# Summing landmark parities on GpSimd from partition-shifted ScalarE copies, in place of two TensorE parity matmuls per batch

## The chip, the cores and the metric

The kernel runs on one core of one Trainium2 chip. The metric is the device time of one execution in microseconds (us). A run counts as slow when it takes over 1.5% longer than the fastest run of the same kernel, and is left out of comparisons. The profile is one execution recorded by the hardware profiler; its span is about 2 us shorter than its quoted time, so I compare spans with spans and times with times.

Engine names as the profile has them: PE is TensorE (matmuls), PEld its weight loads, DVE is VectorE, ACT is ScalarE, POOL is GpSimd, SP is SyncE.

## The reference, cut to what matters

```python
B, H, S, D, m = 8, 8, 576, 64, 32              # batches, heads, rows, head size, landmarks
q_lm = q.reshape(B, H, m, S // m, D).mean(axis=3)      # landmark = mean of 18 consecutive rows
k_lm = k.reshape(B, H, m, S // m, D).mean(axis=3)
A, Bm, C = sm(q, k_lm), sm(q_lm, k_lm), sm(q_lm, k)    # sm: scaled scores, softmax
Z = ...                                        # six iterations towards an inverse of Bm
x = A @ Z @ C @ v                              # as [4608, 512]
out = (((x @ w1) * (x @ w2)) @ w3) @ w_out
```

The inputs are fp32, and so is the output, [4608, 512].

## The kernel before: the parts that the change touches

A tile `qkT` holds q and k with the head dimension and the *parity of the row* along the 128 partitions: partitions 0 to 63 have the even rows and 64 to 127 the odd ones. Each landmark averages even and odd rows, so two steps make it: sums along the free axis (`landmarks`, on GpSimd), and one addition of the two partition halves. The kernel before does this addition on TensorE, at the head of `attention`. It splits the fp32 sums into an fp16 high and low part, multiplies both by a stacked identity `iit`, and ScalarE casts the product to `lm`.

```python
    def landmarks(st, t, eng=nc.gpsimd, pieces=iter(())):
        # ... x = st["qkT"][:, t, hs, :, :]: free-axis sums, six halves and thirds
        eng.tensor_tensor(out=tr, in0=x[:, :, 0, :], in1=x[:, :, 1, :], op=ALU.add)   # L183
        eng.tensor_tensor(out=tr, in0=tr, in1=x[:, :, 2, :], op=ALU.add)              # L184
        eng.tensor_tensor(out=o, in0=t3[:, :, :, 0], in1=t3[:, :, :, 1], op=ALU.add)  # L189
        eng.tensor_tensor(out=o, in0=o, in1=t3[:, :, :, 2], op=ALU.add)               # L190
        eng.tensor_copy(out=hi, in_=o)                                                # L191
        eng.tensor_tensor(out=lo, in0=o, in1=hi, op=ALU.subtract)                     # L192

    def attention(st, bank=None):
        psL = small()
        for i in range(2):
            nc.tensor.matmul(psL[:, :], iit..., parts[:, i]..., ...)                  # L201
        nc.scalar.copy(out=lm, in_=pl)                                                # L206
        nc.gpsimd.tensor_tensor(out=qbd, in0=lm..., in1=par..., op=ALU.mult)          # L208
        yield
        psB = bank()
        # ... first product of two landmark tiles, psB <- lm, lm                      # L217
        # ... (cut: scores, softmaxes, six iterations)
        psZ = small()                                                                 # L404
        # ... psZ <- xd, bmbd
        nc.scalar.activation(out=zt[:, 0], in_=pzv, func=AXF.Copy, scale=-ZS)         # L409
        nc.vector.scalar_tensor_tensor(out=zt[:, 1], in0=pzv, ...)
        normalise(1)                     # VectorE writes the second ahat             # L370
        yield
        # expanded products psG <- zt, wup (L425), evicted to gt by ScalarE (L429) and VectorE
    def up(st, j, w):                    # matmul gt x ahat (L439) into a big() of PSUM (3 buffers)
        # w == 0: ScalarE evicts it to a_sb (L443); w == 1: VectorE multiplies it with a_sb
    def down(ab, b0, t0, half, hold, bank):   # matmuls (L457); ScalarE evicts to o_sb (L466)

    for b in range(B):
        for j in range(8):
            up(st, j, 0); steps(at, (1, 1, 1, 0, 1, 0, 1, 0)[j]); up(st, j, 1)   # cut
        nxt = attention(sts[b + 2], acc)
        for n in range(nd):              # nd = 8 for even b, 10 for odd b
            down(...)
            steps(at)                    # batch b+1's attention proceeds between down products
        steps(at, 30)
        at = nxt
```

At the program's start, PE also multiplies two weights, w3 and w_out: it turns (transposes) blocks of w3 (`w3f`), ScalarE and VectorE evict them as high and low parts (`w3t`, L495 and L496), and PE multiplies these (L503). To *evict* means to copy a product out of PSUM, where PE leaves it.

In these traces each engine takes its instructions in program order, so what stands at the head of an engine's queue delays all that follow on it: the `w3t` eviction that VectorE starts at 26.77 us before the change starts at 30.07 after it, when the sums put in front of it have ended. I call the end of a batch and the beginning of the next the *batch change*. There are six of them in the steady state (those with `b + 2 < B`), three after 8 down steps and three after 10.

The softmax here doesn't subtract the row's maximum and nothing guards it: scores larger than these inputs give would overflow.

## Time and profile before

| before | value | read from |
|---|---|---|
| time, median of 3 | 283.61 us (283.22 to 288.74, the last a slow run) | timed runs |
| span of the profiled run | 281.0 us | profile page |
| PE busy | 269.0 us, 96% | profile page |
| PE on the chain that ended last | 84% | profile page |
| PE's listed waits | 6.5 us, 1.6 of them pauses marked "issue" | list of waits |

The page of the kernel before gives the span, the busy time of each engine (share of the span, number of instructions) and the chain of work that ended last, by engine:

```profile
span 281.0 us, 9504 instructions
...
PE 269.0 (96%) x3996; PEld 152.0 (54%) x3996; DVE 161.8 (58%) x423; ACT 128.9 (46%) x235; POOL 161.7 (58%) x210
...
PE 84%; POOL 4%; ACT 4%; issue 3%; DVE 1%; DMA 1%; ACTq 0%; DVEq 0%; POOLq 0%
```

PE bounds this kernel: it is nearly always busy, and the last work to end hangs on it. The other engines are busy about half the time, but whether they can take more depends on the place. PE's list of waits, before (engine, line, releaser: total us, times, longest us):

```profile
PE big L439 <- ACT a_sb L443: 1.4, 7, 0.2
PE acc L328 <- issue: 1.3, 1, 1.3
...
PE small L201 <- POOL parts L191: 0.8, 1, 0.8
```

In the steady state PE waits only in short stretches of 0.2 us for `a_sb`. The wait for `parts`, and a second of 0.4 us just behind it, are at the start, near 34 us, where the first landmarks come late.

ScalarE's timeline of one batch change, before (start us, duration us, engine, line, operation, out<-in, and in brackets the idle time ahead of it):

```profile
200.89 0.60 ACT L466 ACTIVATE o_sb<-acc 128x512 f32<-128x512 f32 x1 [2.11 <-PE acc L457]
201.38 0.27 ACT L409 ACTIVATE zt<-small 128x128 f16<-128x128 f32 x1
...
205.02 1.02 ACT L429 ACTIVATE gt<-big 128x1024 f16<-128x1024 f32 x1
206.04 0.64 ACT L443 CAST a_sb<-big 128x576 f16<-128x576 f32 x1
```

Although ScalarE is only 46% busy, two short passages have no gap: `zt` starts 0.49 us after an `o_sb` eviction that takes 0.60 us (the two overlap), and the first `a_sb` starts as the last `gt` ends. PE's timeline of the same batch change:

```profile
200.78 0.44 PE L404 MATMUL small<-bmbd,xd 128*64 128x128 f32 x4
...
205.34 0.66 PE L439 MATMUL big<-ahat,gt 128*128 128x288 f16 x4
205.84 0.59 PE L201 MATMUL small<-parts,iit 128*128 128x512 f16 x2
206.27 1.14 PE L439 MATMUL big<-ahat,gt 128*128 128x288 f16 x8
207.34 0.22 PE L217 MATMUL acc<-lm 64*32 64x32 f16 x8
```

The two parity matmuls (L201) occupy PE from 205.84 to 206.27, 0.43 us. This listing also defines the *stage*, from the start of `psZ` (L404, 200.78) to the first landmark product (L217, 207.34). It is 6.56 us here, and has two parts: to the first up product (205.34), 4.56 us, and from there to the landmark product, 2.00 us.

### The profile page before, as it was taken

The numbers are of one execution on the slowest core, as the hardware profiler recorded it, in microseconds if no ns is written. First come the engines' busy times: TensorE is split into PE (matmuls) and PEld (weight loads), VectorE is DVE, ScalarE is ACT, GpSimd is POOL, SyncE is SP. The second block draws the span as 40 slices with busy tenths as digits, with TensorE's granted clock in tenths as the row PEclk, the third lists the DMA queues.
The fourth block names the chain that finished last, engine by engine and source line by source line (L and its number), as shares of the span: only waits on it lengthen the run. The fifth ranks groups of instructions, "written<-read, shape, count | busy, mean of one in ns | idle before, by whom it ended". The sixth has DMA issues, their size and how long they took to land.

```text
span 281.0 us, 9504 instructions
## 1 busy us (share of the span) xinstructions
PE 269.0 (96%) x3996; PEld 152.0 (54%) x3996; DVE 161.8 (58%) x423; ACT 128.9 (46%) x235; POOL 161.7 (58%) x210
## 2 busy tenths in 40 slices
PE   7999899999999998999999999999999999999993
PEld 3456355444673475447645754574468346734741
DVE  7743134644476675656765765576576755766710
ACT  2643245133662574157427732672276246615531
POOL 1717935396279749944897599459947953500000
PEclk9999999999999999999999999999999999999997
DMA  7999999999717996997699969995999452014024
GB/s 220 322 229 252 203 279 161 161 273 160 128 36 158 224 187 103 160 250 160 134 179 228 159 143 213 227 163 112 222 176 160 124 157 77 5 40 109 6 75 112
DMA packets 61979, 45.57 MB, mean 162 GB/s; under 512 B 35569, under 2 KB 54001, under 8 KB 61937
## 3 DMA queue, kind: packets, MB, share of 16 engines
q1 hardware_dynamic: 47280, 31.93, 48.5%
q0 software_dynamic: 13824, 11.54, 29.8%
q10 hardware_dynamic: 832, 1.51, 1.6%
q8 instruction: 31, 0.51, 0.8%
q14 instruction: 12, 0.09, 0.1%
HBM read 38.80 MB, written 9.44 MB: 172 GB/s over the span
## 4 chain that ended last, share of the span: by engine, by line
PE 84%; POOL 4%; ACT 4%; issue 3%; DVE 1%; DMA 1%; ACTq 0%; DVEq 0%; POOLq 0%
PE big L439 23%; PE acc L457 13%; PE big L457 11%; PE acc L503 10%; PE big L382 6%; PE big L425 5%; ACT a_sb L443 2%; PE small L323 2%; PE big L367 2%; PE acc L323 2%; PE big L490 2%; PE big L242 2%; PE small L503 1%; DMA w3f<-in_moe_w_dram 1%; PE big L292 1%
## 5 line engine op out<-in xcount | busy, mean ns | idle before, releaser
L439 PE MATMUL big<-ahat,gt 128*128 128x288 f16 x512 | 72.2, 286 | 2.0 <-ACT a_sb L443 1.4
L445 DVE TENSOR_TENSOR ab<-a_sb,big 128x576 f16<-128x576 f16 x64 | 48.0, 750 | 27.6 <-PE big L439 15.2
L439 PEld LDWEIGHTS <-gt 128*128 128x128 f16 x512 | 48.4, 98 | 20.3 <-issue 5.6
L443 ACT CAST a_sb<-big 128x576 f16<-128x576 f32 x64 | 40.9, 639 | 32.0 <-PE big L439 31.9
L503 PE MATMUL acc<-wsp,w3t 128*128 128x512 f16 x168 | 40.5, 379 | 0.8 <-ACT w L506 0.5
L457 PE MATMUL acc<-w,ab 128*128 128x512 f16 x160 | 40.3, 381 | 0.0
L457 PEld LDWEIGHTS <-ab 128*128 128x128 f16 x288 | 24.0, 98 | 29.0 <-issue 4.2
L457 PE MATMUL big<-w,ab 128*128 128x512 f16 x128 | 32.7, 381 | 0.0
L466 ACT ACTIVATE o_sb<-acc 128x512 f32<-128x512 f32 (+1 forms) x20 | 11.7, 587 | 42.2 <-PE acc L457 40.6
L183 POOL TENSOR_TENSOR tr<-qkT 128x768 f32<-128x768 f16 x16 | 26.3, 1642 | 7.3 <-DMA qkT<-qkn 7.3
L253 POOL TENSOR_TENSOR t<-ect 96x384 f32<-96x384 f32 x16 | 15.9, 995 | 24.3 <-ACT ect L246 16.3
L503 PEld LDWEIGHTS <-w3t 128*128 128x128 f16 x192 | 18.1, 98 | 20.6 <-issue 1.8
L431 DVE TENSOR_SCALAR gt<-big 128x1024 f16<-128x1024 f32 x16 | 19.6, 1225 | 14.8 <-PE big L425 14.8
L184 POOL TENSOR_TENSOR tr<-tr,qkT 128x768 f32<-128x768 f32 x16 | 26.3, 1642 | 1.3
L208 POOL TENSOR_TENSOR qbd<-lm,par 128x512 f16<-128x512 f16 x8 | 8.3, 1042 | 26.3 <-ACT lm L206 26.3
L429 ACT ACTIVATE gt<-big 128x1024 f16<-128x1024 f32 x16 | 16.4, 1025 | 11.9 <-PE big L425 11.9
L496 DVE SCALAR_TENSOR_TENSOR w3t<-big,w3t 128x512 f16<-128x512 f32 x16 | 11.0, 690 | 17.1 <-ACT w3t L495 17.1
L466 ACT ACTIVATE o_sb<-big 128x512 f32<-128x512 f32 x16 | 9.6, 597 | 18.5 <-PE big L457 18.5
L425 PE MATMUL big<-wup,zt 64*32 64x512 f16 x512 | 17.4, 380 | 0.1
L495 ACT ACTIVATE w3t<-big 128x512 f16<-128x512 f32 x16 | 9.5, 594 | 11.8 <-PE big L490 11.8
L246 ACT ACTIVATE ect<-big 96x768 f32<-96x768 f32 x16 | 12.9, 807 | 3.6 <-PE big L242 2.9
L190 POOL TENSOR_TENSOR o<-o,tr 128x256 f32<-128x256 f32 x16 | 12.9, 807 | 1.3
(317 smaller groups left out, 373.0 us busy)
## 6 DMA issues: line engine op xcount, KB each, us to landing
vt<-in_v_dram SPq DMA_DIRECT2D x28, 288.0 KB, 4.3
out_dram<-o_sb SPq DMA_DIRECT2D x23, 192.0 KB, 3.6
qkn<-in_k_dram POOLq DMA_DIRECT2D x12, 288.0 KB, 5.7
qkn<-in_q_dram POOLq DMA_DIRECT2D x12, 288.0 KB, 6.2
w3f<-in_moe_w_dram SPq DMA_DIRECT2D x6, 512.0 KB, 7.8
out_dram<-o_sb SPq DMA_DIRECT2D x24, 128.0 KB, 3.5
wup<-in_moe_w_dram POOLq DMA_DIRECT2D x4, 512.0 KB, 32.9
out_dram<-o_sb SPq DMA_DIRECT2D x24, 64.0 KB, 3.5
```

The costliest lines, as they stand in the source:

```text
L183: eng.tensor_tensor(out=tr, in0=x[:, :, 0, :], in1=x[:, :, 1, :], op=ALU.add)
L184: eng.tensor_tensor(out=tr, in0=tr, in1=x[:, :, 2, :], op=ALU.add)
L382: nc.tensor.matmul(psI[32 * t:32 * t + 32, qd, o:96], tz_[sl, qd, :], sz_[sl, qd, o:96], start=True, stop=True, tile_position=(32 * h, 32 ...
L425: nc.tensor.matmul(psG[32 * h:32 * h + 32, qd, :], zt[rs, i, h, :], wup[rs, h, w, fs], start=(i == 0), stop=(i == 1), tile_position=(64 * ...
L429: nc.scalar.activation(out=g[:, :, w, fs], in_=psG, func=AXF.Copy, scale=1.0 / ZS)
L431: nc.vector.tensor_scalar(out=g[:, :, w, fs], in0=psG, scalar1=1.0 / ZS, scalar2=None, op0=ALU.mult)
L439: nc.tensor.matmul(p[:, c, 0:HS], st["g"][:, qd, w, 128 * j:128 * j + 128], st["ahat"][qd][:, c, :], start=(qd == 0), stop=(qd == 1))
L443: nc.scalar.copy(out=st["a_sb"], in_=p[:, :, 0:HS])
L445: nc.vector.tensor_tensor(out=st["ab"][:, j, st["t0"]:st["t0"] + S].rearrange("p (c s) -> p c s", c=2), in0=st["a_sb"], in1=p[:, :, 0:HS], ...
L457: nc.tensor.matmul(pso[:, :], ab[:, j, t0:t0 + 128], w34[:, j, :], start=(j == 0), stop=(j == 7))
L466: nc.scalar.activation(out=o_sb[:, c], in_=pso[:, c], func=AXF.Copy, scale=1.0 / (X64 * X64))
L503: nc.tensor.matmul(psW[j][:, :], turned[j, c // 4][:, a, c % 4, :], wsp[:, b, c, :], start=(c == 0 and a + b == 0), stop=(c == 7 and a == 1))
```

## The change

The intent is to take the parity matmuls off the busiest engine. Two ScalarE copies swap the partition halves of the fp32 sums into a tile `far`, and one GpSimd addition `o + far` gives `lm` at once, in both halves. The high/low split, the PSUM tile and the cast from PSUM go. The shifts are placed where the sums are ready: k after the sixth `down` of a batch, q at the batch's end. At the start, VectorE takes half of the heads of batch 0's q sums from GpSimd, which was late there.

The core of the diff, with cuts marked:

```diff
-            eng.tensor_copy(out=hi, in_=o)
-            eng.tensor_tensor(out=lo, in0=o, in1=hi, op=ALU.subtract)
+    def sums(st, t, shared=False, pieces=iter(())):
+        # ... o = st["o"][t], the four additions as before
+        work = ((nc.gpsimd, 0, 4), (nc.vector, 4, 4)) if shared else ((nc.gpsimd, 0, H),)
+        # ...
+    def landmarks(st, t):
+        o = st["o"][t]
+        far = pz.tile([128, H, 32], FP32, name="far", bufs=1)
+        nc.scalar.copy(out=far[0:64], in_=o[64:128])
+        nc.scalar.copy(out=far[64:128], in_=o[0:64])
+        # ...
+        nc.gpsimd.tensor_tensor(out=lm[:, t], in0=o, in1=far, op=ALU.add)
+        if t == 0:  # ... qbd as before
@@ attention
-        psL = small()
-        for i in range(2):
-            nc.tensor.matmul(psL[:, :], iit..., parts[:, i]..., ...)
-        nc.scalar.copy(out=lm, in_=pl)
@@ start
-        landmarks(sts[0], 0)
+        sums(sts[0], 0, shared=True)
         load_w3(5)
         steps(fd, 4)
+        landmarks(sts[0], 1)
         # ...
-        steps(fd, 6)
+        steps(fd, 3)
+        landmarks(sts[0], 0)
+        steps(fd, 4)
@@ batch loop
-        nxt = attention(sts[b + 2], acc) if b + 2 < B else iter(())
         for n in range(nd):
             # ... down(...)
+            if b + 2 < B and n == 5:
+                landmarks(sts[b + 2], 1)
             steps(at)
         steps(at, 30)
-        at = nxt
+        if b + 2 < B:
+            landmarks(sts[b + 2], 0)
+            at = attention(sts[b + 2], acc)
```

More of the change, by code (lines that the diff above doesn't have):

```diff
@@ L137, in constants @@
         eye = consts.tile([128, 2, 32], FP32, name="eye")
-        iit = consts.tile([128, 2, 64], FP16, name="iit")
         onesq = consts.tile([128, 2, 4, 2, 4], FP16, name="onesq")
@@ L146, in constants @@
             nc.vector.memset(par[sl, i:i + 1], 1.0)
-            for jj in range(2):
-                nc.vector.tensor_copy(out=iit[sl, jj, :], in_=ident[sl, sl])
         for h in range(4):
@@ L171, in constants @@
         nc.vector.tensor_tensor(out=eye2, in0=eye, in1=eye, op=ALU.add)
-        return mask4, par, ones, eye2, iit, onesq, selc, lomask
-    def landmarks(st, t, eng=nc.gpsimd, pieces=iter(())):
-        if "parts" not in st:
-            st["parts"] = pz.tile([128, 2, 2, H, 32], FP16, name="parts")
-        for h0 in ((0,) if eng is nc.gpsimd else (0, 4)):
-            own, n = ("", H) if eng is nc.gpsimd else ("v", 4)
+        return mask4, par, ones, eye2, onesq, selc, lomask
+    def sums(st, t, shared=False, pieces=iter(())):
+        if "o" not in st:
+            st["o"] = {}
+        o = st["o"][t] = pz.tile([128, H, 32], FP32, name="o%d" % t, bufs=1)
+        work = ((nc.gpsimd, 0, 4), (nc.vector, 4, 4)) if shared else ((nc.gpsimd, 0, H),)
+        for eng, h0, n in work:
+            own = "" if eng is nc.gpsimd else "v"
             hs = slice(h0, h0 + n)
             x = st["qkT"][:, t, hs, :, :]
-            tr = pat.tile([128, n, NP], FP32, name="tr" + own, bufs=1)
+            tr = pat.tile([128, 4 if own else H, NP], FP32, name="tr" + own, bufs=1)[:, 0:n]
             eng.tensor_tensor(out=tr, in0=x[:, :, 0, :], in1=x[:, :, 1, :], op=ALU.add)
@@ L186, in landmarks @@
             t3 = tr.rearrange("p h (l g) -> p h l g", g=3)
-            o = pat.tile([128, n, 32], FP32, name="o3" + own, bufs=1)
-            hi, lo = st["parts"][:, 0, t, hs, :], st["parts"][:, 1, t, hs, :]
-            eng.tensor_tensor(out=o, in0=t3[:, :, :, 0], in1=t3[:, :, :, 1], op=ALU.add)
-            eng.tensor_tensor(out=o, in0=o, in1=t3[:, :, :, 2], op=ALU.add)
-            eng.tensor_copy(out=hi, in_=o)
-            eng.tensor_tensor(out=lo, in0=o, in1=hi, op=ALU.subtract)
-            next(pieces, None)
+            eng.tensor_tensor(out=o[:, hs], in0=t3[:, :, :, 0], in1=t3[:, :, :, 1], op=ALU.add)
@@ new lines, in sums @@
+            eng.tensor_tensor(out=o[:, hs], in0=o[:, hs], in1=t3[:, :, :, 2], op=ALU.add)
+            next(pieces, None)
+    def landmarks(st, t):
[3 more added lines that the diff above has]
+        nc.scalar.copy(out=far[64:128], in_=o[0:64])
+        if "lm" not in st:
+            st["lm"] = pat.tile([128, 2, H, 32], FP16, name="lm")
+        lm = st["lm"]
+        nc.gpsimd.tensor_tensor(out=lm[:, t], in0=o, in1=far, op=ALU.add)
+        if t == 0:
+            qbd = st["qbd"] = pat.tile([128, H, 2, 32], FP16, name="qbd")
+            nc.gpsimd.tensor_tensor(
+                out=qbd,
+                in0=lm[:, 0, :, :].unsqueeze(2).to_broadcast([128, H, 2, 32]),
+                in1=par.unsqueeze(1).unsqueeze(3).to_broadcast([128, H, 2, 32]),
+                op=ALU.mult)
@@ L196, in attention @@
     def attention(st, bank=None):
         bank = bank or small
-        qkT, vt, parts = st["qkT"], st["vt"], st["parts"]
-        psL = small()
-        for i in range(2):
-            nc.tensor.matmul(psL[:, :], iit.rearrange("p a d -> p (a d)"),
-                             parts[:, i].rearrange("p t h l -> p (t h l)"),
-                             start=(i == 0), stop=(i == 1))
-        pl = psL.rearrange("p (t h l) -> p t h l", t=2, l=32)
-        lm = pat.tile([128, 2, H, 32], FP16, name="lm")
@@ L206, in attention @@
-        nc.scalar.copy(out=lm, in_=pl)
-        qbd = pat.tile([128, H, 2, 32], FP16, name="qbd")
-        nc.gpsimd.tensor_tensor(
-            out=qbd,
-            in0=lm[:, 0, :, :].unsqueeze(2).to_broadcast([128, H, 2, 32]),
-            in1=par.unsqueeze(1).unsqueeze(3).to_broadcast([128, H, 2, 32]),
-            op=ALU.mult)
-        yield
+        qkT, vt, lm, qbd = st["qkT"], st["vt"], st["lm"], st["qbd"]
         psB = bank()
@@ L576 @@
         load_weight(1, moe_w2)
-        mask4, par, ones, eye2, iit, onesq, selc, lomask = constants()
+        mask4, par, ones, eye2, onesq, selc, lomask = constants()
         fd = fold(pf, wof, w3f, wsp, warm_up)
@@ L593 @@
         turn_on_pe(sts[0], 1, 4, nc.vector.tensor_copy)
-        landmarks(sts[0], 1)
+        sums(sts[0], 1)
         steps(fd, 5)
@@ L597 @@
         turn_on_pe(sts[0], 0, 4, nc.vector.tensor_copy)
-        landmarks(sts[0], 0)
+        sums(sts[0], 0, shared=True)
         load_w3(5)
         steps(fd, 4)
+        landmarks(sts[0], 1)
         load_w3(6)
         turn_all(1)
-        steps(fd, 6)
+        steps(fd, 3)
+        landmarks(sts[0], 0)
+        steps(fd, 4)
         at = attention(sts[0])
-        for n, m in enumerate((2, 2, 2, 3, 3, 2, 1, 1, 1, 1, 2, 2, 3, 3)):
+        for n, m in enumerate((2, 2, 3, 3, 2, 2, 1, 1, 1, 2, 2, 3, 3)):
             steps(at)
-            if n == 1:
+            if n == 0:
                 load_w3(7)
-            elif n == 4:
+            elif n == 3:
                 pieces = qk_pieces(sts[2], 2)
-                landmarks(sts[1], 1, pieces=pieces)
-                landmarks(sts[1], 0, pieces=pieces)
-            if 3 < n < 8:
-                load_v_piece(sts[1], 1, n - 4, ident[0:NP, 0:1])
+                sums(sts[1], 1, pieces=pieces)
+                sums(sts[1], 0, pieces=pieces)
+            if 2 < n < 7:
+                load_v_piece(sts[1], 1, n - 3, ident[0:NP, 0:1])
             steps(fd, m)
         steps(at, 30)
+        landmarks(sts[1], 1)
+        landmarks(sts[1], 0)
         steps(fd, 64)
@@ L631 @@
             up(st, j, 0)
-            steps(at, (1, 1, 1, 0, 1, 0, 1, 0)[j])
+            steps(at, (0, 1, 1, 0, 1, 0, 1, 0)[j])
             if b + 2 < B and j > 5:
@@ L637 @@
                 pieces = qk_pieces(sts[b + 3], b + 3) if b + 3 < B else iter(())
-                landmarks(sts[b + 2], 1, pieces=pieces)
-                landmarks(sts[b + 2], 0, pieces=pieces)
+                sums(sts[b + 2], 1, pieces=pieces)
+                sums(sts[b + 2], 0, pieces=pieces)
         steps(at, 1)
-        nxt = attention(sts[b + 2], acc) if b + 2 < B else iter(())
         hold = {}
```

## The prediction

> **What bounds it now.** TensorE: busy 269.0 of the 281.0 us span (the page), 84% of the chain that ended last. PE's waits on other engines sum to about 6 us (list of waits). Only PE time, or a new PE wait, counts. ScalarE (46%), VectorE and GpSimd (58%) have slack on average, not at each place.
>
> **What goes, comes, moves.**
> - PE: two 128x512 parity matmuls per batch go. In the timeline they push the next matmul from 205.84 to 206.27: 0.43 us, 3.4 us in eight batches.
> - ScalarE: the 595 ns lm cast goes; four 64x256 shifts per batch come, of which the trace has none. The Trainium skill ("ScalarE: Activation LUTs", What ACT_TABLE_LOAD costs) gives 186 ns + 0.833 ns per element, neighbours overlapping by 93 ns; the trace's 96x1 copy at 183 ns agrees. Estimate: 0.4 us each, 0.7 us a pair.
> - GpSimd: per parity 397 + 672 ns (cast, subtract) go, one add (about 0.67 us) comes.
> - VectorE: half the q sums of batch 0, about 1.5 us once.
>
> **Start.** PE waited 0.77 + 0.37 us for the sums at 34 us. Now they should be ready about 33.4, and PE needs them about 34.4: 1.57 us gained with the two matmuls. But the w3 block that PE turns at 41.75 was issued at 23.5 and took 17.8 us, landing about 41.3; an earlier PE then waits. I count 0.9 (0.5 to 1.5). Batch 1, shifted well ahead, gains its 0.43.
>
> **Steady state: 0.43 gained, more given back, at two places in each of six batch changes.**
> 1. The k shifts stand between an o_sb eviction and zt on ScalarE. zt slips from 201.38 to about 202.0; VectorE takes zt, then ahat, in order, so the second ahat ends about 203.25, not 202.63. The second expanded product (L425) takes its PSUM buffer, at 202.86: a new PE wait near 0.4 us.
> 2. The q shifts stand before the first a_sb of the next batch. Chain: shifts 0.7, GpSimd add 0.67, first landmark product. After an 8-chunk batch a_sb slips about 0.6 us, and the third up product needs its buffer: PE reaches the landmark product about 0.4 us later than before, the removed matmuls counted. After a 10-chunk batch that product waits for the add: about 0.24 us later.
> Sum: 3 x (0.42 + 0.37) + 3 x (0.42 + 0.24) = about 4.3 us lost.
>
> **Net.** -0.9 - 0.4 + 4.3 = +3; shaded, since waits may overlap, to +2.3. Predicted 285.9 us against 283.6; eight times in ten 282.4 to 288.6. Faster by over 2%: 0.01; within 2%: 0.94; slower by over 2%: 0.05.
>
> **What would show each step.**
> - PE busy falls by about 3.4 us or more, yet the span doesn't; the list of waits gains PE waits behind ScalarE's a_sb, VectorE's ahat and GpSimd's lm, 0.2 to 0.9 us each, six times ahat, three each the others.
> - Shifts near 0.4 us, pairs just ahead of zt and of a batch's first a_sb in ScalarE's timeline.
> - The first landmark product 0.2 to 0.4 us later after the last down product.
> - At 34 us no PE wait for GpSimd; perhaps one for w3f near 40 us.
>
> **What would make it wrong.** Shifts much shorter than 0.4 us: both steady waits fade, and the kernel gains about 3 us. Slack at ahat that I don't see would do half of that. Shifts or adds slowed by shared SBUF traffic (VectorE and GpSimd summing together at the start) would make it worse; the landing of w3f decides the start.

## More of the kernel before

The line numbers shift: L404, L409, L425, L439, L443, L457, L466, L217 and L496 of before are L401, L406, L422, L436, L440, L454, L463, L214 and L493 after. The shifts are L193 and L194, the addition L198, and the sums L182 to L187.

## The result, and the profile after

The changed kernel took 291.01, 290.81 and 291.43 us in three fast runs and 302.56 us in a slow one (clock 0.975), median of all four 291.22 us. The kernel before took a median of 283.71 us in the same rounds. Ratios here and below are the mean time of one kernel's fast runs over that of the other's of the same rounds, so not quite the ratio of the medians that I quote. The ratio is 1.0266, 95% interval 1.0241 to 1.029: slower by over 2%, and outside the predicted range.

The page after:

```profile
span 289.2 us, 9473 instructions
...
PE 268.8 (93%) x3980; PEld 150.1 (52%) x3980; DVE 164.6 (57%) x423; ACT 138.4 (48%) x259; POOL 155.1 (54%) x194
...
PE 72%; ACT 10%; DVE 5%; POOL 5%; issue 4%; DMA 1%; ACTq 0%; POOLq 0%; DVEq 0%
```

PE has fallen from 84% of the chain to 72%, and ScalarE, VectorE and GpSimd have taken its place. ScalarE's busy share rose by only two points. PE's list of waits, after:

```profile
PE big L436 <- ACT a_sb L440: 4.0, 10, 0.9
PE acc L214 <- POOL lm L198: 2.9, 3, 1.0
PE acc L500 <- DVE w3t L493: 2.0, 2, 1.7
PE big L422 <- DVE ahat L367: 1.5, 6, 0.3
PE big L422 <- ACT zt L406: 1.5, 6, 0.2
```

What is new comes in threes and sixes, at the six batch changes: of the ten waits for `a_sb`, seven are the short ones of before, and three, of 0.86 us each, are new. The `w3t` wait is at the start. ScalarE's timeline of the same batch change, after:

```profile
204.87 0.60 ACT L463 ACTIVATE o_sb<-acc 128x512 f32<-128x512 f32 x1 [2.11 <-PE acc L454]
205.49 0.40 ACT L193 COPY far<-o 64x256 f32<-64x256 f32 x1
205.90 0.41 ACT L194 COPY far<-o 64x256 f32<-64x256 f32 x1
206.33 0.28 ACT L406 ACTIVATE zt<-small 128x128 f16<-128x128 f32 x1
...
209.87 1.02 ACT L426 ACTIVATE gt<-big 128x1024 f16<-128x1024 f32 x1
210.92 0.40 ACT L193 COPY far<-o 64x256 f32<-64x256 f32 x1
211.34 0.40 ACT L194 COPY far<-o 64x256 f32<-64x256 f32 x1
211.76 0.64 ACT L440 CAST a_sb<-big 128x576 f16<-128x576 f32 x1
```

Both passages without a gap have been cut open. `zt` now starts 1.46 us after `o_sb`, where it was 0.49: the pair of copies inserts 0.97 us. The first `a_sb` starts 0.87 us after `gt` ends, where it was 0. Look at the starts: each copy begins only when what stands before it has ended (204.87 + 0.60 = 205.47, and the copy starts at 205.49), and `zt` after it likewise. PE's timeline, after:

```profile
204.76 0.44 PE L401 MATMUL small<-bmbd,xd 128*64 128x128 f32 x4
...
206.66 0.74 PE L422 MATMUL big<-wup,zt 64*32 64x512 f16 x16 [0.24 <-ACT zt L406]
207.65 0.63 PE L422 MATMUL big<-wup,zt 64*32 64x512 f16 x16 [0.25 <-DVE ahat L367]
...
212.45 0.65 PE L436 MATMUL big<-ahat,gt 128*128 128x288 f16 x4 [0.86 <-ACT a_sb L440]
213.03 0.22 PE L214 MATMUL acc<-lm 64*32 64x32 f16 x8
```

The stage is now 8.27 us (213.03 - 204.76). The parity matmuls have gone, and three waits have come.

The start of the program, VectorE's timeline after:

```profile
26.22 0.89 DVE L182 TENSOR_TENSOR trv<-qkT 128x384 f32<-128x384 f16 x1
27.14 1.07 DVE L183 TENSOR_TENSOR trv<-trv,qkT 128x384 f32<-128x384 f32 x1
28.24 0.92 DVE L186 TENSOR_TENSOR o<-trv 128x128 f32<-128x128 f32 x1
29.20 0.95 DVE L187 TENSOR_TENSOR o<-o,trv 128x128 f32<-128x128 f32 x1
30.07 1.28 DVE L493 SCALAR_TENSOR_TENSOR w3t<-big,w3t 128x512 f16<-128x512 f32 x2
```

The four shared sums take 3.83 us of VectorE's time, where I had estimated 1.5 us, and the `w3t` eviction behind them starts at 30.07 us; before, it started at 26.77. PE waits 1.74 us for it at 30.81. So the waits for `parts` went, as predicted, and one of 1.74 us, where they were 1.1 us together, came about four microseconds earlier.

Where the time went, from these timelines (the stage is the median of three batch changes of each kind; first entry after 8 down steps, second after 10):

| | before | after | change | predicted |
|---|---|---|---|---|
| to the first up product of batch 0 | 71.34 us | 70.99 us | -0.35 | -0.9 |
| first up to landmark product, batch 1 | 2.00 | 1.57 | -0.43 | -0.43 |
| stage, six batch changes | 6.56 / 8.29 | 8.27 / 9.76 | 3 x (1.71 + 1.47) = +9.5 | +4.3 |

Of the first -0.35, 0.19 us is an earlier first product that the change has no part in (7.27 us instead of 7.46), so the start gained about 0.16. The sum is +8.7 us. PE's unexplained pauses marked "issue" outside these stretches sum to 1.6 us before and 1.1 us after, and such pauses vary from run to run; that leaves 8.2, and the spans differ by 8.2. The steady state is therefore the question: it lost twice what I had predicted.

### The profile page after: what moved, and what is told of

It reads as the page before. It is cut to its first block, busy times and chain, and to the rows that moved or that the text cites. A ratio compares the mean times of both kernels' runs of the same rounds, so it can differ in the third digit from the quotient of the medians.

```text
span 289.2 us, 9473 instructions
## 1 busy us (share of the span) xinstructions
PE 268.8 (93%) x3980; PEld 150.1 (52%) x3980; DVE 164.6 (57%) x423; ACT 138.4 (48%) x259; POOL 155.1 (54%) x194
## 4 chain that ended last, share of the span: by engine, by line
PE 72%; ACT 10%; DVE 5%; POOL 5%; issue 4%; DMA 1%; ACTq 0%; POOLq 0%; DVEq 0%
PE big L436 18%; PE acc L500 12%; PE acc L454 11%; PE big L454 8%; PE big L379 5%; PE big L422 3%; ACT a_sb L440 3%; ACT o_sb L463 2%; PE small L320 2%; PE big L487 2%; PE small L500 2%; ACT far L194 2%; ACT far L193 2%; PE big L239 2%; PE acc L320 1%
## 5 line engine op out<-in xcount | busy, mean ns | idle before, releaser
L436 PE MATMUL big<-ahat,gt 128*128 128x288 f16 x512 | 72.0, 286 | 4.8 <-ACT a_sb L440 4.0
L436 PEld LDWEIGHTS <-gt 128*128 128x128 f16 x512 | 48.2, 98 | 22.8 <-issue 9.3
L440 ACT CAST a_sb<-big 128x576 f16<-128x576 f32 x64 | 40.6, 639 | 34.5 <-PE big L436 34.4
L454 PE MATMUL acc<-w,ab 128*128 128x512 f16 x160 | 40.3, 381 | 0.0
L454 PEld LDWEIGHTS <-ab 128*128 128x128 f16 x288 | 24.0, 98 | 28.9 <-issue 4.1
L454 PE MATMUL big<-w,ab 128*128 128x512 f16 x128 | 32.7, 381 | 0.0
L198 POOL TENSOR_TENSOR lm<-o,far 128x256 f16<-128x256 f32 x16 | 11.7, 730 | 37.5 <-ACT far L194 36.4
L463 ACT ACTIVATE o_sb<-acc 128x512 f32<-128x512 f32 (+1 forms) x20 | 11.7, 586 | 41.6 <-PE acc L454 38.9
L182 POOL TENSOR_TENSOR tr<-qkT 128x768 f32<-128x768 f16 (+1 forms) x16 | 25.8, 1609 | 8.0 <-DMA qkT<-qkn 7.8
L183 POOL TENSOR_TENSOR tr<-tr,qkT 128x768 f32<-128x768 f32 (+1 forms) x16 | 25.6, 1597 | 1.3
L422 PE MATMUL big<-wup,zt 64*32 64x512 f16 x512 | 18.8, 381 | 3.0 <-DVE ahat L367 1.5
L463 ACT ACTIVATE o_sb<-big 128x512 f32<-128x512 f32 x16 | 9.6, 597 | 21.5 <-PE big L454 21.5
L493 DVE SCALAR_TENSOR_TENSOR w3t<-big,w3t 128x512 f16<-128x512 f32 x16 | 10.9, 686 | 13.3 <-ACT w3t L492 13.3
L422 PEld LDWEIGHTS <-zt 64*32 64x32 f16 x512 | 6.1, 89 | 15.3 <-issue 7.5
```

What stands on the lines that cost most here:

```text
L422: nc.tensor.matmul(psG[32 * h:32 * h + 32, qd, :], zt[rs, i, h, :], wup[rs, h, w, fs], start=(i == 0), stop=(i == 1), tile_position=(64 * ...
L436: nc.tensor.matmul(p[:, c, 0:HS], st["g"][:, qd, w, 128 * j:128 * j + 128], st["ahat"][qd][:, c, :], start=(qd == 0), stop=(qd == 1))
L440: nc.scalar.copy(out=st["a_sb"], in_=p[:, :, 0:HS])
L454: nc.tensor.matmul(pso[:, :], ab[:, j, t0:t0 + 128], w34[:, j, :], start=(j == 0), stop=(j == 7))
L463: nc.scalar.activation(out=o_sb[:, c], in_=pso[:, c], func=AXF.Copy, scale=1.0 / (X64 * X64))
```

## The experiments

**The theory.** The two places named in the prediction are the right ones, and the loss is larger because the copies overlap nothing: not each other, not the eviction before them, not the eviction behind them. I had let every neighbour overlap by 93 ns. The cause of the lost overlap is that the copies start at another partition than their neighbours.

**Rivals.** (a) The loss comes from elsewhere, for instance memory traffic, and moving the shifts would not recover it. (b) The copies fail to overlap because they depend on each other or on the same tile, whatever the partitions. (c) Copies of 64 partitions never overlap. For the start: (d) VectorE's sums are simply that slow, or (e) VectorE and GpSimd slow each other when both add.

Eleven experiments ran, nine new kernels and two repeats, in three groups; those of a group share one chip and the runs of the kernel before (medians 282.26, 282.16 and 283.06 us). All passed the comparison with the reference, also the two that compute wrong landmarks; so that comparison does not notice a wrong landmark half here, and says little of this step.

### k_early: the k shifts moved ahead of `zt`'s passage

```diff
-            if b + 2 < B and n == 5:
+            if b + 2 < B and n == 4:
                 landmarks(sts[b + 2], 1)
```

> The changed kernel, with the k shifts of batches 2 to 7 issued one half down-product earlier (before the o_sb eviction, where ScalarE is idle, not between it and zt). Theory (place on ScalarE): the wait at zt and at the second ahat goes, about 0.87 us in each of six batches, 5.2 us in all: about 286.0 us, ratio to the kernel before about 1.008; no PE wait on zt or ahat in the list of waits. Rival (the shifts and the GpSimd add cost the same wherever they stand, by their number or by shared SBUF traffic): stays at about 291, 1.026.

Measured: 288.31 us (286.68 to 289.5), ratio 1.0214, 1.0137 to 1.0291. This misses the expected 1.008, and the interval contains the rival's 1.026, so the time alone does not decide between them; the trace does. Stage 7.40 / 8.90 us; the part to the first up product is back to 4.55 / 6.29 us as before the change. The `zt` and `ahat` waits are gone from the list, and the `a_sb` and `lm` waits stand unchanged (4.0 and 2.9 us). So the k place is settled: 0.87 us for each batch change. The profile also shows where the time went: the first up product of batch 0 comes at 72.78 us, 1.8 us later than in the changed kernel, behind two pauses marked "issue" of 0.9 us each that lie ahead of anything the edit moves. From there to the end the run takes 212.9 us instead of 218.2: 5.3 us less, where 5.2 were expected. What causes these pauses is open, and the other three runs have no profile.

### q_early: the q shifts moved ahead of the first `a_sb`

```diff
-        far = pz.tile([128, H, 32], FP32, name="far", bufs=1)
+        far = pz.tile([128, H, 32], FP32, name="far")
@@
             steps(at)
+            if b + 2 < B and n == 5:
+                landmarks(sts[b + 2], 0)
         steps(at, 30)
         if b + 2 < B:
-            landmarks(sts[b + 2], 0)
             at = attention(sts[b + 2], acc)
```

> The changed kernel, with the q shifts of batches 2 to 7 issued right behind zt (ScalarE idle until gt), not at the end of the batch; far gets a second buffer. Theory (place): the a_sb and lm waits at the batch change go, 3 x 0.84 + 3 x 0.61 = 4.4 us: about 286.8 us, ratio about 1.011. The zt wait stays. Rival (cost by number): 291, 1.026.

Measured: 285.19 us (284.31 to 289.3, the last a slow run), ratio 1.0089, 1.0026 to 1.0152. Stage 7.38 / 8.72 us: the part behind the first up product fell from 2.86 / 2.61 to 1.97 / 1.56 us, and the other part stayed (5.41 / 7.16). The mirror image of k_early, as the theory has it. The second buffer of `far` is not what did it: in the changed kernel the addition that reads `far` ended at 207.63 us, long before the q copies start at 210.92.

### both_early: both moves

The edit is the sum of the last two.

> Both moves together. Theory: the two sites add up, 9.6 us gone: about 281.6 us, ratio about 0.993, faster than the kernel before by about the 0.43 us per batch of the parity matmuls less the loss at the start. Rival: 291. If the sites are not independent (ScalarE full between zt and gt), between 283 and 286.

Measured: 280.26 us (279.86 to 280.55), ratio 0.9924, 0.9874 to 0.9974. Stage 6.52 / 7.86 us. This takes back the whole steady loss and falls below the kernel before in the 10-step changes, by 0.43 us, the removed matmuls' time. Rival (a) is out: with the same instructions and the same traffic, place alone decides. ScalarE's timeline shows why it costs nothing now:

```profile
196.28 0.40 ACT L193 COPY far<-o 64x256 f32<-64x256 f32 x1
...
198.37 0.60 ACT L463 ACTIVATE o_sb<-acc 128x512 f32<-128x512 f32 x1 [1.27 <-PE acc L454]
198.86 0.27 ACT L406 ACTIVATE zt<-small 128x128 f16<-128x128 f32 x1
```

The k copies stand in front of 1.27 us of idle time, and `zt` again starts 0.49 us after `o_sb`; the q copies start at 199.56, behind `zt`, after 0.43 us of idle time.

In the 8-step changes the removed matmuls gain only 0.04 us. There PE's 12 up matmuls start at 202.86 us and the landmark product follows at 204.83. The first `a_sb` frees the buffer that the third up product needs, and it runs from 203.56 to 204.20, right behind `gt`. So PE reaches the wait for that buffer earlier and waits longer. I read this from the trace and did not test it by an experiment.

### two_unshifted: two copies of the same time, without a change of start partition

Two copies of 128 partitions, out of and into partition 0; the landmarks are wrong. One copy of 128x256 should take as long as one of 64x256, for it has as many elements per partition.

```diff
-        nc.scalar.copy(out=far[0:64], in_=o[64:128])
-        nc.scalar.copy(out=far[64:128], in_=o[0:64])
+        nc.scalar.copy(out=far2[:, 0], in_=o)
+        nc.scalar.copy(out=far2[:, 1], in_=o)
```

> Wrong result on purpose: at the same places, in the same number, each copy takes all 128 partitions to the same partitions (into two halves of a double tile), so no copy starts at partition 64; columns per copy stay 256. Theory (a copy that changes its start partition does not overlap its neighbours on ScalarE, which is what my 0.1 us overlaps missed): copies overlap again by 0.1 us at each seam, the insertion before zt falls from 0.97 to about 0.6 us and before a_sb from 0.87 to about 0.5, so about 4.4 us of 9.6 come back: about 286.8 us, ratio 1.011. Rival (the overlap is missing for another reason, such as SBUF as the source or 256 columns): stays near 291, copies still end to end in the timeline.

ScalarE's timeline at `zt`'s passage:

```profile
201.62 0.60 ACT L464 ACTIVATE o_sb<-acc 128x512 f32<-128x512 f32 x1 [2.11 <-PE acc L455]
202.11 0.40 ACT L193 COPY far<-o 128x256 f32<-128x256 f32 x1
202.41 0.41 ACT L194 COPY far<-o 128x256 f32<-128x256 f32 x1
202.71 0.28 ACT L407 ACTIVATE zt<-small 128x128 f16<-128x128 f32 x1
```

The copies take the same 0.40 us each, but now they follow each other at 0.30 us and overlap on both sides. `zt` starts 1.09 us after `o_sb`: the insertion is 0.60 us, the prediction's own number, where the shifted pair inserts 0.97. Rival (b) is weakened: these copies too share their tiles and are in the same order.

The stage is 7.54 / 9.15 us. By its parts, as loss against before:

| place | predicted | two_unshifted | after |
|---|---|---|---|
| `zt`, each change | +0.42 | +0.49 | +0.86 |
| `a_sb` and `lm`, 8 steps | +0.37 | +0.48 | +0.85 |
| `lm`, 10 steps | +0.24 | +0.37 | +0.61 |
| six changes, from the stages | +4.3 us | +5.5 us | +9.5 us |

So the lost overlap is 9.5 - 5.5 = 4.0 us, out of the 5.2 us by which the steady loss was underestimated. The other 1.2 us are 0.07 to 0.13 us at each place, spread evenly; one part of them is the GpSimd addition, 0.73 us where I had taken 0.67, and I have not separated the rest.

The timed result was 288.14 us (286.29 to 291.55), ratio 1.0182, 1.0093 to 1.0271. The two lowest runs (286.3) agree with the expected 286.8; 289.94 does not, and 291.55 is a slow run. The interval contains the expected 1.011.

### own_half: two half copies that stay in their halves

The landmarks are wrong here as well.

```diff
-        nc.scalar.copy(out=far[0:64], in_=o[64:128])
-        nc.scalar.copy(out=far[64:128], in_=o[0:64])
+        nc.scalar.copy(out=far[0:64], in_=o[0:64])
+        nc.scalar.copy(out=far[64:128], in_=o[64:128])
```

> Wrong result on purpose: the changed kernel, with each copy kept inside its own partition half (0 to 63, then 64 to 127), so nothing crosses but the second copy starts at partition 64. If a change of start partition against the neighbour is what ends the overlap: the first copy starts 0.1 us before the o_sb eviction ends, the second and zt do not overlap; zt starts about 1.33 us after o_sb does (unshifted 1.09, shifted 1.46). If only reading and writing different halves ends it: as unshifted, 1.09.

```profile
205.38 0.60 ACT L463 ACTIVATE o_sb<-acc 128x512 f32<-128x512 f32 x1 [2.11 <-PE acc L454]
205.87 0.39 ACT L193 COPY far<-o 64x256 f32<-64x256 f32 x1
206.27 0.40 ACT L194 COPY far<-o 64x256 f32<-64x256 f32 x1
206.70 0.28 ACT L406 ACTIVATE zt<-small 128x128 f16<-128x128 f32 x1
```

The first copy, from partition 0 to partition 0, starts before `o_sb` has ended (205.97). The second, from 64 to 64, waits for the first to end, and `zt`, which writes from partition 0, waits for the second. `zt` starts 1.32 us after `o_sb`, between the unshifted 1.09 and the shifted 1.46, and close to the 1.33 expected. All six batch changes show the same, and the stage, 8.13 / 9.62 us, lies between those of two_unshifted and of the changed kernel. Rival (c) is out: a 64-partition copy does overlap when its start partition agrees with its neighbour's. Rival (b) is out too: `zt` shares no tile with the copies and is held as well, while in two_unshifted two copies into one tile overlap. At the other place the first copy, at partition 0, did not overlap `gt` (it started at 211.28, as `gt` ended); the copy that had last read SBUF before it had started at partition 64. So what counts is not always the direct neighbour. No run has two copies in a row that both start at partition 64, so whether these would overlap is not shown.

The Trainium skill ("VectorE: DVE Perf Modes", Two Vector instructions with no wait between them) states such a rule for VectorE, as a model: an instruction whose input starts in another quadrant of 32 partitions than the last read of the same memory, or whose output starts in another than the last write to it, is held until earlier ones have finished. It does not state it for ScalarE. On ScalarE, the starts of the copies and of what follows them in these three kernels agree with it.

### both_unshared and both_deferred: the start

Both build on both_early. both_unshared leaves all of batch 0's q sums to GpSimd; both_deferred keeps VectorE's half, but issues it behind the two `w3t` evictions.

```diff
-        sums(sts[0], 0, shared=True)              # both_unshared
+        sums(sts[0], 0)
```
```diff
-        sums(sts[0], 0, shared=True)              # both_deferred
+        sums(sts[0], 0, shared=True, part=0)      # GpSimd's half
         load_w3(5)
         steps(fd, 4)
+        sums(sts[0], 0, shared=True, part=1)      # VectorE's half
```

> Both shifts moved early, and the q sums of batch 0 wholly on GpSimd again (no VectorE half). Theory of the start: VectorE's four sums took 3.9 us beside GpSimd and held the third-matrix eviction (w3t) back, so TensorE waited 1.4 to 1.7 us near 30 us; without them this wait is gone, and GpSimd alone still has the landmarks ready when TensorE needs them. Against the run with both shifts moved: 1.0 to 1.6 us less, ratio to the kernel before about 0.988. Rival (sharing was needed: GpSimd alone is late by 1 us or more, as before the change): TensorE waits for lm near 34 us instead and the time is the same, 0.992.

> Both shifts moved early, sharing kept, but VectorE's half is issued behind the two w3t evictions that it held up. Theory: the 1.4 to 1.7 us wait for w3t near 30 us goes, as in the unshared run, about 0.988. Rival: VectorE's late half now delays the landmarks and TensorE waits for lm near 34 us; the time stays at 0.992.

Measured: both_unshared 278.54 us (277.99 to 280.7), ratio 0.9893, 0.9815 to 0.9972; both_deferred 278.08 us (277.47 to 279.42), ratio 0.9858, 0.9794 to 0.9921. In both, PE's wait for `w3t` falls from 1.6 us in both_early to 0.2 us, the value of before, and no wait for `lm` takes its place. With the parity steps removed, GpSimd alone has `lm` at 33.86 us and PE needs it at 34.39. So the sharing of the sums was not needed, and in the changed kernel's order it cost about what it was meant to gain. The intervals tell these two kernels apart neither from each other nor from both_early (0.9874 to 0.9974). The gain is read from the profiles: the first up product comes at 68.81 and 68.98 us, where it came at 71.48 in both_early behind an "issue" pause of 1.1 us, which leaves 1.6 and 1.4 us.

### dead_sums: the shared sums measured by themselves

both_early, with VectorE's four sums done once more near 50 us, where GpSimd idles from 44.7 to 52.8 us; the results are not used.

> Both shifts moved early, plus the four VectorE sums of batch 0's q once more into scratch near 50 us, where GpSimd waits for its data. Theory (VectorE and GpSimd slow each other when both read two SBUF inputs): the four take about 0.5, 0.5, 0.3, 0.3 us there against 0.6 to 0.9, 1.1, 0.9, 0.4 to 0.95 beside GpSimd. Rival (these shapes are simply slow on VectorE, for instance the three-apart reads): the same durations as beside GpSimd.

VectorE's timeline in the idle stretch:

```profile
49.23 0.54 DVE L611 TENSOR_TENSOR trd<-qkT 128x384 f32<-128x384 f16 x1
49.80 0.56 DVE L612 TENSOR_TENSOR trd<-trd,qkT 128x384 f32<-128x384 f32 x1
50.40 0.33 DVE L614 TENSOR_TENSOR od<-trd 128x128 f32<-128x128 f32 x1
```

With the fourth, 0.33 us again, they take 1.76 us in all, close to my estimate of 1.5. In the same run, beside GpSimd's sums, the same four take 0.91, 1.15, 0.92 and 0.45 us, 3.43 in all. Theory (e) holds, and (d) is out. GpSimd suffers as well: its first half-size sum takes 1.11 us beside VectorE in the changed kernel, and 0.91 in both_deferred, where VectorE's sums come later.

The Trainium skill ("SBUF — State Buffer", SBUF: two separate sides) says how: VectorE operations with two SBUF inputs, and GpSimd operations that read SBUF, share a pair of SBUF ports under an exclusive lock, and the one that comes second "fully blocks". GpSimd's timeline at the start of the changed kernel agrees:

```profile
26.06 0.63 POOL L186 TENSOR_TENSOR o<-tr 128x256 f32<-128x256 f32 x1
26.77 1.02 POOL L187 TENSOR_TENSOR o<-o,tr 128x256 f32<-128x256 f32 x1
27.87 1.11 POOL L182 TENSOR_TENSOR tr<-qkT 128x384 f32<-128x384 f16 x1
29.05 0.91 POOL L183 TENSOR_TENSOR tr<-tr,qkT 128x384 f32<-128x384 f32 x1
```

These end at 26.69, 27.79, 28.98 and 29.96 us, and VectorE's four sums, shown above, at 27.11, 28.21, 29.16 and 30.15: each 0.42, 0.42, 0.18 and 0.19 us later, always a little less than the lone durations. The engines take turns. This reading of the turns is from one trace; the slowing itself is shown by the experiment.

### after_again and shifts_on_dve

The changed kernel once more, as a control in the third group, and a version of it whose shifts VectorE makes, in the same places.

```diff
-        nc.scalar.copy(out=far[0:64], in_=o[64:128])
-        nc.scalar.copy(out=far[64:128], in_=o[0:64])
+        nc.vector.tensor_copy(out=far[0:64], in_=o[64:128])
+        nc.vector.tensor_copy(out=far[64:128], in_=o[0:64])
```

> Control: the changed kernel unaltered, on the chip of these runs. 1.0266 on the first chip; expected 1.025 to 1.035 here.

> The changed kernel with the four shifts per batch at the same points of the program, but on VectorE. Theory (what costs is the place in ScalarE's queue, ahead of zt and a_sb, not the shifting): VectorE waits 1.9 us for zt anyway, so the zt wait goes (0.87 us in six batches); at the change of batch a_sb is no longer held, but after 8-chunk batches the chain shift, add, first landmark product still ends about 0.8 us late (VectorE has its gt eviction first), after 10-chunk batches it is in time. About 3 x 0.8 - 3 x 0.4 = +1.2 us in the six batches, and near 0.5 us gained before: ratio 1.000 to 1.006. Rival (shifting across halves costs on any engine): 1.02 or more.

Measured: after_again 294.43 us (292.16 to 294.97), ratio 1.038, 1.0327 to 1.0434, with the same stages, 8.27 / 9.76 us. This is above the expected 1.025 to 1.035, and slower than in the first comparison by more than the intervals allow. The stages don't hold the difference. In the profile the start holds most of it: the first up product comes at 74.13 us instead of 70.99, which is 3.1 us of the 3.5 by which the spans differ (292.7 and 289.2). Of these, 1.7 us are 13 `w3t` matmuls that took 4.67 us instead of 2.98, in a stretch (20 to 40 us) where the granted clock was 0.91 and not 1.00, and 0.9 us is one "issue" pause. Why clock and pauses differ is open.

shifts_on_dve 285.04 us (284.45 to 286.51), ratio 1.0077, 1.0037 to 1.0118, a little above what was expected. It rules out the rival's 1.02. The copies take 0.29 us each on VectorE with GpSimd idle, but up to 0.88 us in five of the six k passages, where GpSimd is at work beside them; in the three where a pair takes longest (1.44 to 1.64 us) the part to the first up product is still 0.50 to 0.70 us longer than before. PE no longer waits for ScalarE's `zt`, its waits for `a_sb` are those of before (1.4 us), but it still waits for `lm`, 2.6 us in three places. So part of the loss comes from the late q addition whichever engine shifts, and part from VectorE and GpSimd slowing each other once more.

### best_again: both_deferred in five rounds

> The version with both shifts moved early and VectorE's half issued behind w3t, once more against the kernel before, in five rounds: 0.984 to 0.989. If the first result was luck of three rounds, above 0.992.

Measured: 278.29 us (277.59 to 279.46), ratio 0.984, 0.9808 to 0.9872, beside 283.06 us of the kernel before: 4.8 us or 1.6% faster, clear of the noise though under 2%, and so faster than both kernels. PE is busy 266.0 us of its 276.5 us span.

## Why the prediction was wrong, point by point

- **What bounds the kernel: right.** Only new PE waits and saved PE time counted. ScalarE's 46% meant nothing at the two passages that have no gap.
- **The two places: right.** The list of waits after names them as predicted: `ahat` six times, `a_sb`, and `lm` three times. At `zt` PE waited twice, 0.24 us for `zt` itself and 0.25 for `ahat`, where I had expected a single wait of 0.4.
- **The step that failed: "Estimate: 0.4 us each, 0.7 us a pair", with "neighbours overlapping by 93 ns".** The single copy is right: 402 ns measured against the 399 ns that I estimate for 256 elements from the formula that the prediction cites (the Trainium skill, "ScalarE: Activation LUTs", What ACT_TABLE_LOAD costs). The overlap is wrong. A shifted pair runs end to end, 0.82 us, and overlaps its outer neighbours neither, so it inserts 0.97 us ahead of `zt` and 0.87 us ahead of `a_sb`. I had counted about 0.6 for either. two_unshifted, which keeps the overlap, shows the predicted insertion of 0.60 us and a steady loss of 5.5 us; own_half shows that the change of start partition is what breaks the overlap. This term is worth 4.0 us.
- **The rest of the steady sum: too small by 1.2 us**, 0.07 to 0.13 us at each place, not settled further.
- **The shading from +3 to +2.3 "since waits may overlap": wrong**, by 0.7 us. The two places lie one behind the other on PE, and k_early and q_early recovered 0.87 and 0.89 us of the 8-step stage independently; both together gave 1.75.
- **The start: too hopeful.** I predicted -0.9 us and got about -0.16. The waits at 34 us went. The `w3f` landing that I had feared near 40 us did not bind, also in both_deferred, where PE is earlier still (its only waits for `w3f` are before 7 us). But "half the q sums of batch 0, about 1.5 us once" was 3.83 us beside GpSimd, and it stood ahead of a `w3t` eviction that PE needed. The prediction named the mutual slowing as a thing that could make it wrong, and did not price it.
- **Batch 1: right**, -0.43 us, as predicted.
- **PE's busy time** did not fall by 3.4 us in the page (269.0 to 268.8). In both_deferred, without the new waits, it is 265.6. Most of the difference is in the list of lines: the expanded products (L425, L422 after) keep PE busy for 17.4 us before and 18.8 after, and the same number of matmuls lasts 380 and 381 ns each, so they do not run longer but follow each other less closely. They take 18.8 us in q_early, which has the waits at `zt`, and 17.4 and 17.0 in k_early and both_early, which have not. Why they spread out behind these waits is not shown.

The terms together: steady +5.2, shading +0.7, start +0.7 is 6.6 us more than predicted, of which the shorter "issue" pauses (0.5) and the earlier first product (0.2) took back 0.7; that makes 5.9, and the spans' 8.2 us exceed the predicted 2.3 by 5.9.

## What to carry to other kernels

Work that leaves the bottleneck engine costs nothing only if it lands in idle time of the engine that takes it, at that place: here the steady state's 24 copies lost 9.5 us in two passages without a gap, and nothing a few instructions earlier or later. Before costing short instructions by a rate with an overlap, ask whether each neighbour pair really overlaps; copies that shift between partitions did not, and that cost 4.0 of the 9.5 us. And two engines that add at the same time may slow each other, as VectorE (3.83 us instead of 1.76 for four sums) and GpSimd did here; then a split of sums is a loss for whatever is queued behind them.

## What the Trainium skill lacked or had wrong

- "ScalarE: Activation LUTs", What ACT_TABLE_LOAD costs: it says that back-to-back ACTIVATEs overlap by about 93 ns, with no condition. Copies from and to partition 0 agree (0.40 us each, 0.30 us from start to start). Copies whose start partition differs from their neighbour's don't overlap: 0.42 us from start to start, and none at either end of the pair.
- "VectorE: DVE Perf Modes", Two Vector instructions with no wait between them: the rule of held instructions is given for VectorE alone. ScalarE's starts in own_half (`zt` 1.32 us behind `o_sb`, against 1.09 unshifted and 1.46 shifted) follow the same rule. No page says so for ScalarE.
- "SBUF — State Buffer", SBUF: two separate sides: the exclusive lock agrees with the trace, but the page gives no size for two-input additions. Here VectorE's 128x384 addition took 0.54 us alone and 0.91 beside GpSimd, its 128x128 addition 0.33 alone and 0.92 beside it, and GpSimd's 128x384 addition 0.91 and 1.11.
